# Own terms of two more units as TensorE products, decay rows first on two queues, and fewer idle products at the start

## The chip, the cores and the metric

The kernel runs on one core of one Trainium2 chip. The time is device microseconds of one execution; three runs of the kernel before took 583.14 to 583.82 us, with a median of 583.75. The engines are TensorE (PE, with its weight loads as PEld), VectorE (DVE), ScalarE (ACT), GpSimd (POOL) and SyncE (SP, which here only issues DMAs).

## What is computed

A recurrent attention block and, on its output, a dense block with the activation h - tanh(h):

```python
batch, n_heads, seq, head_dim = (4, 8, 768, 48)
for t in range(S):
    kt, vt, rt = (k[:, :, t], v[:, :, t], r[:, :, t])
    cur = np.einsum('bhd,bhe->bhde', u[None] * kt, vt)
    y[:, :, t] = np.einsum('bhd,bhde->bhe', rt, state + cur)
    state = w[None, :, :, None] * state + np.einsum('bhd,bhe->bhde', kt, vt)
...
n_tokens, d_model, d_ff = (3072, 384, 2048)
h = x @ w_in
g = h - np.tanh(h)
return (g @ w_out).astype(np.float32)
```

The term with `u` is the own term: the part of a step's output that comes from that step's own k and v.

## The kernel before

**Units.** The recurrence is cut into 24 units. Unit n covers a chunk of 64 steps (`SHORT`) of two of the four batches (`ch, half = divmod(n, 2)`), 128 rows in all. Per unit, r and k are transposed on PE (`turn`), scaled by powers of the decay w on DVE or ACT (`rT`, `kT`), and multiplied to a table `at` of step against step (`levels`, 16 products of 64x64). DVE copies the part before the diagonal into `at` by a mask (`x.cp`, line 830). The diagonal of `at` is the own term. PE then multiplies `at` by v (`outputs`), and `kw` (k times the decay to the chunk's end, `w_down`) by v to the new state (`to_state`). The result goes to `xt` and `rest`, the input of the dense block. The first two units have no state before them and take a shorter way.

**The own term has two ways.** Where `n < OWN` (line 32; OWN is 1), ACT scales `kT` by `w_u` in four operations (`own_k`, line 709), PE makes 16 products of it with `rT` (`own_levels`), and DVE copies their diagonal into `at` with the mask `same` (line 821). Else DVE makes `rk = r * k` (line 696), multiplies it by `ub`, a copy of u on all partitions (line 824), and sums it per head to `du` (line 700); ACT writes eight diagonals `same * du` into `at` (`diagonal`, line 704).

**The start.** w and u are loaded as eight short rows (`rows`, line 547) and transposed on PE into columns (line 549). ACT keeps a copy (`saved`, line 563). DVE makes the decay's powers from the columns: `by` (line 552), a scan to `power` (554), a reciprocal to `inverse` (558), which the scaling of r and k reads. `table` (line 529) transposes the inverse powers, and ACT makes `w_down` from it (562). POOL makes `w_u` and checks the bounds of w. `warm` (line 572) is an activation whose only use is that the table of ACT's functions is loaded. The weights come as 64-bit floating-point words in pieces of 768 KB (`st`) and are converted on DVE and ACT (lines 185 to 191).

**Idle products.** `fills` (line 534) are products of the identity with itself that write a bank which nobody reads: 512 columns for number 0, 256 for number 1, and the same two in another bank for numbers 2 and 3. They only keep PE busy.

**The dense block.** A block of two units gives 256 tokens; for each block and each pair of the 16 tiles of 128 columns of `w_in`, PE makes `h`, ACT and DVE make `g` from it by five activations (`th`, `s`, `sq`, `small`, `tg`) and three vector operations, and PE multiplies `g` by `w_out`, in the later passes by seven products instead of eight (`products`, line 307).

**What sets the order.** `lay_out` lists every piece of work as a task of one engine, and the string `ORDER` (line 45) names the tasks one by one, two characters each; numbers past the last task are idle products. `written` emits them in that order. So `ORDER` fixes what each engine, and each engine's DMA queue, does after what; an engine waits in place for what its next instruction needs.

Of the kernel before, what the change touches and what calls it, by code (L numbers as in the profile page):

```python
# [1279 lines left out]
```

## Time and profile before

| | |
|---|---|
| median of three runs | 583.75 us |
| the profiled execution | 583.45 us |
| its span, first instruction to last | 581.5 us |
| instructions | 14198 |
| granted TensorE clock, mean | 0.994 |
| PE busy | 567.1 us (98%) |
| DVE, ACT, POOL busy | 429.1, 403.5, 203.3 us |
| DMA | 38.48 MB |

The page of the profile gives the busy time of each engine and the chain of work that ended last: from the last instruction back to what released each one. In order of time, a row is: start, duration, engine, line, operation, out<-in, size, how many were merged, and in brackets the idle time before it with what ended it. Starts of neighbours on an engine are closer than their durations, since neighbours overlap. An idle product counts as busy time. A product of 32-bit numbers shows as two in the trace (x32 for 16 products of `levels`), a transpose as one.

### The profile page before, as it was taken

The numbers are of one execution on the slowest core, as the hardware profiler recorded it, in microseconds if no ns is written. First come the engines' busy times: TensorE is split into PE (matmuls) and PEld (weight loads), VectorE is DVE, ScalarE is ACT, GpSimd is POOL, SyncE is SP. The second block draws the span as 40 slices with busy tenths as digits, with TensorE's granted clock in tenths as the row PEclk, the third lists the DMA queues.
The fourth block names the chain that finished last, engine by engine and source line by source line (L and its number), as shares of the span: only waits on it lengthen the run. The fifth ranks groups of instructions, "written<-read, shape, count | busy, mean of one in ns | idle before, by whom it ended". The sixth has DMA issues, their size and how long they took to land.

```text
span 581.5 us, 14198 instructions
## 1 busy us (share of the span) xinstructions
PE 567.1 (98%) x5493; PEld 482.1 (83%) x5493; DVE 429.1 (74%) x720; ACT 403.5 (69%) x925; POOL 203.3 (35%) x366
## 2 busy tenths in 40 slices
PE   6899999999999999999999999999999999999997
PEld 3577777677777699999898889899899998989996
DVE  3799868699999989658789878686775564463545
ACT  2599899979777675637758776876776576765651
POOL 5003211110100144455357254446264344463340
PEclk7999999999999999999999999999999999999999
DMA  9966256776341001133343454423232010010001
GB/s 173 182 143 113 54 113 133 183 145 157 71 97 52 1 1 27 29 55 61 46 75 73 70 88 70 63 37 65 41 56 39 1 34 4 5 24 2 14 23 32
DMA packets 138548, 38.48 MB, mean 66 GB/s; under 512 B 130760, under 2 KB 132904, under 8 KB 138472
## 3 DMA queue, kind: packets, MB, share of 16 engines
q1 hardware_dynamic: 130140, 29.71, 27.9%
q0 software_dynamic: 4992, 6.99, 5.3%
q10 hardware_dynamic: 3340, 0.79, 0.8%
q8 instruction: 45, 0.74, 0.5%
q14 instruction: 31, 0.25, 0.1%
HBM read 31.66 MB, written 4.72 MB: 63 GB/s over the span
## 4 chain that ended last, share of the span: by engine, by line
PE 88%; DVE 4%; DMA 3%; ACT 2%; issue 2%; SPq 1%; POOL 1%; ACTq 0%; DVEq 0%
PE h L217 42%; PE p L307 27%; PE o L254 10%; PE yk_ps L606 6%; PE h L534 1%; PE x_ps L656 1%; SPq L644 1%; DMA vt<-in_v_dram 1%; DMA xt<-rest 1%; DMA first_k<-in_k_dram 1%; PE x_ps L606 1%; PE p L254 0%; ACT xt L765 0%; ACT rest L765 0%; DVE at L830 0%
## 5 line engine op out<-in xcount | busy, mean ns | idle before, releaser
L217 PE MATMUL h<-xt,w_in_sb 128*128 128x256 f32 x1152 | 266.4, 381 | 1.5 <-DMA xt<-rest 0.7
L217 PEld LDWEIGHTS h<-xt,w_in_sb 128*128 128x128 f32 x1152 | 214.9, 190 | 34.3 <-issue 2.3
L290 POOL TENSOR_TENSOR sg<-g 128x256 f32<-128x256 f32 x69 | 56.8, 824 | 169.8 <-DVE g L246 137.4
L242 DVE TENSOR_TENSOR g<-h,th 128x512 f32<-128x512 f32 x96 | 65.8, 686 | 60.2 <-ACT tg L233 29.1
L229 ACT ACTIVATE s<-h 128x512 f32<-128x512 f32 x96 | 57.3, 597 | 59.0 <-PE h L217 45.6
L307 PE MATMUL p<-mixed,sg 128*128 128x192 f32 x426 | 92.1, 326 | 0.0
L244 DVE TENSOR_TENSOR tg<-s,tg 128x512 f32<-128x512 f32 x96 | 69.1, 721 | 25.2 <-ACT s L224 17.7
L246 DVE COPY_PREDICATED g<-small,tg 128x512 f32<-128x512 int32 x96 | 73.0, 765 | 15.8 <-ACT small L235 12.9
L233 ACT ACTIVATE tg<-h 128x512 f32<-128x512 f32 x96 | 57.0, 594 | 33.0 <-PE h L217 29.0
L231 ACT ACTIVATE th<-h 128x512 f32<-128x512 f32 x96 | 56.5, 593 | 32.5 <-PE h L217 31.9
L307 PEld LDWEIGHTS p<-mixed,sg 128*128 128x128 f32 x426 | 73.5, 190 | 1.3 <-POOL sg L292 0.3
L307 PE MATMUL p<-w_out_sb,g 128*128 128x192 f32 x284 | 70.2, 329 | 0.0
L235 ACT ACTIVATE small<-s,smallb 128x512 f32<-128x512 f32 x96 | 68.5, 721 | 1.3
L254 PE MATMUL o<-w_out_sb,g 128*128 128x384 f32 x192 | 66.5, 489 | 0.5 <-DVE g L246 0.3
L786 POOL DMA_DIRECT2D xt<-rest x66 | 32.8, 502 | 94.7 <-ACT rest L765 94.7
L224 ACT ACTIVATE s<-s 128x512 f32<-128x512 f32 x96 | 60.3, 632 | 1.2
L254 PEld LDWEIGHTS o<-w_out_sb,g 128*128 128x128 f32 x192 | 35.6, 190 | 21.2 <-ACT parts L278 0.7
L307 PEld LDWEIGHTS p<-w_out_sb,g 128*128 128x128 f32 x284 | 50.7, 190 | 2.6
L704 ACT ACTIVATE at<-same,du 128x64 f32<-128x64 f32 x184 | 47.6, 341 | 6.5 <-PE yk_ps L606 5.0
L292 POOL TENSOR_TENSOR sg<-sg,g 128x128 f32<-128x128 f32 x69 | 39.4, 575 | 3.3
L294 POOL TENSOR_TENSOR sg<-sg,g 128x128 f32<-128x128 f32 x69 | 38.4, 561 | 3.9
L345 POOL DMA_DIRECT2D out_dram<-o x44 | 23.9, 545 | 39.8 <-DVE o L339 23.0
(126 smaller groups left out, 670.9 us busy)
## 6 DMA issues: line engine op xcount, KB each, us to landing
st<-in_moe_w_out_dram SPq DMA_DIRECT2D x8, 768.0 KB, 5.2
st<-in_moe_w_in_dram SPq DMA_DIRECT2D x16, 288.0 KB, 4.7
rt<-in_r_dram SPq DMA_DIRECT2D x46, 96.0 KB, 3.0
vt<-in_v_dram SPq DMA_DIRECT2D x46, 96.0 KB, 3.0
kt<-in_k_dram SPq DMA_DIRECT2D x44, 96.0 KB, 3.3
out_dram<-o POOLq DMA_DIRECT2D x44, 96.0 KB, 2.3
st<-in_moe_w_in_dram POOLq DMA_DIRECT2D x16, 96.0 KB, 5.5
parts<-in_k_dram SPq DMA_DIRECT2D x48, 32.0 KB, 2.2
```

Source lines behind the costliest of these rows:

```text
L217: self.nc.tensor.matmul(t.h2[:, z], self.w_in_sb[:, t.f // 2, kk, z * 128 : (z + 1) * 128], self.xts[t.j][:, kk].rearrange("p b t -> p (b ...
L224: A.activation(t.s, t.s, AF.Square, scale=G3)
L229: A.activation(out, t.h, AF.Arctan, scale=G2)
L231: A.activation(out, t.h, AF.Tanh)
L233: A.activation(out, t.h, AF.Tanh, scale=G1)
L235: A.activation(out, t.s, AF.Relu, bias=self.smallb, scale=-1.0)
L242: V.tensor_tensor(t.g, t.h, t.th, ALU.subtract)
L244: V.tensor_tensor(t.tg, t.s, t.tg, ALU.mult)
L246: V.copy_predicated(t.g, t.small.bitcast(I32), t.tg)
L254: self.nc.tensor.matmul(self.outs[i], t.g2[:, z, i * C : (i + 1) * C], self.w_out_sb[:, t.f + z, :], start=t.first and z == 0, stop=t.last ...
L290: add(t.s4[:, :2], g[:, 0::3], g[:, 1:2].to_broadcast([128, 2, C]), ALU.add)
L307: self.nc.tensor.matmul(ps[bank][:, half * n : (half + 1) * n], a, b, start=t.first and half == 0, stop=t.last, skip_group_check=True)
```

## The change

`OWN` goes from 1 to 3, and `ORDER` is replaced as a whole; nothing else is changed, except that all lines after it move up by one.

```diff
 PASSES = 4, 4, 8
-OWN = 1
+OWN = 3
 SWAP = 2
...
 ORDER = (
-    "0F2m2i2j2k2f2g2h00012l2n0J0K0G0H0IbWbW2q323133bX022o033534362t040A3738390C060U050B0T2s070V2rbWbWbWbW082u09bX2v2p"
...
+    "00010H2f2j2i2k2g2h0J2m2l2nbSbT020A030I040C060KbSbSbSbT2q0B2o3231333534362s050d072r2ubSbS2x2t0V2y2v082w090L3A0M2p"
...
```

With OWN at 3, units 1 and 2 take the first way of the own term, which unit 0 took already. The table has 18 idle fills before (nine of number 0, seven of 1, two of 2) and ten after (six of 0, three of 1, one of 3). Three places show the rest of what is moved; rows are in the order of the engine's program, without times.

At the very start, PE and ACT. `x_ps_146` is the bank of unit 0 and `x_ps_150` that of unit 1; `h<-ident` are fills. PE before, from its first instruction:

```order
L534 MATMUL h<-ident 128x512 x2
L656 MATMUL x_ps_146<-ident,first_k_122 128x128 x4
L534 MATMUL h<-ident 128x256
L549 MATMUL yk_ps<-ident,rows 128x8
L656 MATMUL x_ps_146<-ident,rt_106 128x128 x4
L534 MATMUL h<-ident 128x512 x4
L529 MATMUL h<-ident,twice 128x128 x4
L534 MATMUL h<-ident 128x256
L606 MATMUL x_ps_146<-rT,kU 64x64 x16
L566 MATMUL h<-one,ok 1x1
L606 MATMUL x_ps_146<-rT,kT 64x64 x16
L656 MATMUL x_ps_150<-ident,rt_107 128x128 x4
```

and PE now:

```order
L533 MATMUL h<-ident 128x512
L533 MATMUL h<-ident 128x256
L548 MATMUL yk_ps<-ident,rows 128x8
L533 MATMUL h<-ident 128x512 x3
L533 MATMUL h<-ident 128x256
L655 MATMUL x_ps_146<-ident,first_k_122 128x128 x4
L655 MATMUL x_ps_146<-ident,rt_106 128x128 x4
L533 MATMUL h<-ident 128x512 x2
L605 MATMUL x_ps_146<-rT,kT 64x64 x16
L605 MATMUL x_ps_146<-rT,kU 64x64 x16
L528 MATMUL h<-ident,twice 128x128 x4
L655 MATMUL x_ps_150<-ident,rt_107 128x128 x4
```

The transpose of w's and u's rows now comes before those of k and r, three fills and a half stand between them, two stand ahead of the levels, and none ahead of `table`. ACT before, from its first instruction (`L644` are loads of r, k and v):

```order
L644 DMA vt_116<-in_v_dram 64x8x48
L644 DMA first_k_122<-in_k_dram 64x8x48
L644 DMA rt_106<-in_r_dram 64x8x48
L547 DMA rows<-in_u_dram 4x2x48
L572 ACT_TABLE_LOAD
L572 ACTIVATE warm<-one 128x1
L644 DMA rt_107<-in_r_dram 64x8x48
L644 DMA first_k_123<-in_k_dram 64x8x48
L563 COPY saved<-yk_ps 128x8
L644 DMA vt_117<-in_v_dram 64x8x48
L560 COPY twice<-inverse 128x512
```

and ACT now:

```order
L546 DMA rows<-in_u_dram 4x2x48
L643 DMA first_k_122<-in_k_dram 64x8x48
L643 DMA rt_106<-in_r_dram 64x8x48
L643 DMA vt_116<-in_v_dram 64x8x48
L562 ACT_TABLE_LOAD
L562 COPY saved<-yk_ps 128x8
L643 DMA rt_107<-in_r_dram 64x8x48
L643 DMA first_k_123<-in_k_dram 64x8x48
L559 COPY twice<-inverse 128x512
```

The row of u is first on ACT's queue, as that of w is first on SP's (where `ub` was first before; it is now the 20th row there, after unit 2's loads). `warm` has left this place for a later one, the table load stands ahead of `saved`, and the second half of unit 1's v (`vt_117`) has moved behind a conversion of weights further down. `saved` also stands before `by` in the whole order now, after it before.

On DVE, from the scaled r of unit 0 to the masked copies of unit 1 (`at_132` is unit 0's table, `at_133` unit 1's; `same` is the mask of the own term). Before:

```order
L830 COPY_PREDICATED at_132<-before,x_ps_146 128x512
L807 TENSOR_TENSOR kw_113<-first_k_123,w_down 128x8x48
L696 TENSOR_TENSOR rk<-rt_107,first_k_123 128x384
L821 COPY_PREDICATED at_132<-same,x_ps_146 128x512
L189 SCALAR_TENSOR_TENSOR w_in_sb<-w_in_sb,st 128x768
L665 TENSOR_TENSOR kT<-x_ps_150,inverse 128x512
L660 TENSOR_TENSOR rT<-x_ps_150,power 128x512
L824 TENSOR_TENSOR rk<-rk,ub 128x384
L700 TENSOR_REDUCE du<-rk 128x8
L190 SCALAR_TENSOR_TENSOR power<-st,power 128x768
L191 TENSOR_TENSOR w_in_sb<-w_in_sb,power 128x768
```

and now:

```order
L820 COPY_PREDICATED at_132<-same,x_ps_146 128x512
L184 TENSOR_SCALAR power<-st 128x768
L185 TENSOR_SCALAR w_in_sb<-st 128x768
L806 TENSOR_TENSOR kw_112<-first_k_122,w_down 128x8x48
L806 TENSOR_TENSOR kw_113<-first_k_123,w_down 128x8x48
L664 TENSOR_TENSOR kT<-x_ps_150,inverse 128x512
L659 TENSOR_TENSOR rT<-x_ps_150,power 128x512
L188 SCALAR_TENSOR_TENSOR w_in_sb<-w_in_sb,st 128x768
L189 SCALAR_TENSOR_TENSOR power<-st,power 128x768
L829 COPY_PREDICATED at_133<-before,x_ps_150 128x512
L190 TENSOR_TENSOR w_in_sb<-w_in_sb,power 128x768
L184 TENSOR_SCALAR power<-st 128x768
```

`rk`, its product with `ub` and `du` are gone for unit 1; after the rows shown come one more conversion and unit 1's copy of the own term. Unit 0's `kw` has moved behind its two masked copies and the first steps of the conversion, which come in the same order as before.

On ACT at the first tile of the dense block, before (`at_132` here is unit 2's table):

```order
L704 ACTIVATE at_132<-same,du 128x64 x8
L233 ACTIVATE tg<-h 128x512
L231 ACTIVATE th<-h 128x512
L229 ACTIVATE s<-h 128x512
L224 ACTIVATE s<-s 128x512
L765 COPY xt<-yk_ps 64x3x64 x4
```

and now:

```order
L708 ACTIVATE kU<-kT,w_u 128x128 x4
L794 ACTIVATE state_127<-yk_ps,power 128x2x48 x4
L186 ACTIVATE power<-power,p_bias 128x768
L187 ACTIVATE st<-st 128x768
L230 ACTIVATE th<-h 128x512
L228 ACT_TABLE_LOAD
L228 ACTIVATE s<-h 128x512
L223 ACTIVATE s<-s 128x512
L234 ACTIVATE small<-s,smallb 128x512
L232 ACTIVATE tg<-h 128x512
L764 COPY xt<-yk_ps 64x3x64 x4
```

Unit 2's eight diagonals are four `kU`, a conversion's two steps and a second load of function tables have come between, and `small` has moved ahead of unit 2's `xt`. Everywhere else the same work stands in another order.

More of the change, by code (lines that the diff above doesn't have):

```diff
@@ new lines @@
+    "0N3C3T3B0D2z3S3U3E0O3D3738390P0S3J2+3G2_3Q0Q3K303H3P3R0R0e3F3V0f0T0U3I3q0g0E3ZbT3L0h3r3s3a3M0i3Y3o893c3n3p3b3d0j"
+    "3N0k3e3O0W3g3W3X0X3f4K0Y8A3h0F0Z3x4L4M8C3y4I0a8B3i4H4J3_8E0l0b8F8D3t400c3w3u3v3j4k8G8L153+4i3z0u3k418M4V423l4W44"
+    "434X4Y4l4m454h4j8H8ObV464R8P4O8I8N4S470m4Q4N4P8J0n3m485E4T8K8Q5B4C494U4v4F5C5D4Z4E4w4a4B4r0o5F5G4A4D4G4b4o0p134x"
+    "4c0w0q4y4s5c8T4d4q5f5P8Z5e5g5Q4e4t4n4p8a4u4f4z5R5b5d8S4+5S5L4g688b8l4_696A5T0r5H508e5I5J0s8R5K518U5M668m5N656752"
+    "6Z8V8d5A535O5p575i8c555q5U8f565l8n5r596V8W588q5V5hbW5j8p8h6Y6a5s8g5W6W6X8r8i5k8X545m5X8z5n6C6F735Y6J8+0t5o5Z7274"
@@ new lines @@
+    "5t6K6B6D5u6L8Y1D8t6M8j5v8_916E926G8o5w956N7S8s6_6j8k5x8u70716f7T7U8v5y6k5a905_6H8w6I605z9362948x647P6O8y96616c63"
+    "6l977Q7R6P6mJw7D6Q6n7E5+JxJy6e6b6d6R796g1L7d99Jt6h6S7eJuJv9A6i7F146T7G6U756o7H9N6p9D9B9E6q76779CKK9G7A6rKLKM7Z78"
+    "K5987f6sK69O7C7B6vKH7g6t6y0v9H6z7W7I7h6x6+9P9Z6w7JKq9FKIKJ9R9I7Y9Q127K7V7X9S9U6u7a7LK79J7b0x7M9a0y7c7N0zKV7iKW0+"
+    "9VJz9K9c7j9LKo0_9TJ+J_7k9d10KrKs9b9n9eKX119f9o7l9g1V16KnKp9z7m171TKS187u9W9+7s9h9M7p197t9X9p7r1AKY7q9i1U9YLB9r1E"
+    "9qKN1FA19jLCLD7O9s1BKOKP9_9k1G9u9v9tAB1C9mA29w1g1fAC9lA51HLh1h1M1WA39xK2A01NLE1OA49yLFLG1IADLiLjAEANA6AF1J1PAOAI"
@@ new lines @@
+    "AGAHAJAbAP1QARAc1KASAT1X1pA7AQKt1Y1R1e1ZA8AU1aAVAnA91bKZAKAoAA1SAfAeAL1xAqAiLkAdAWAMLlLmAg1cArAhA_K_1dApAsB0Au23"
+    "24AtAjM626BBAkB2KuKvB1Av25B4BCAwB31q0GAXB6BF1rBE1sBPBI1iAZB71tBQ1jBD1u1kAY1vB5BGBbB8Aa1w1lAlBT2P1mBSBcBH1nAm1oBe"
+    "BRLP2E2FBUAxBJ2G2HM5M7BKBdAyBgBWBf1yBVBXBpBhBYBiBq1z27B_AzBrA+Bt281+B9Bj1_BABs20Mc29C0MbMd21Bu2ABxBLBwBkCDBNC322"
+    "BvBMC12I2XC2CEC6BO2BCPCG2JCQ2C2KLQC4BZ2D2LByK8Ba2MCHC52NBlCFCKCSBm2QK92OCdC7BnCRBoCeCIC8CJ2YCUBz2ZCVCLCT2RB+2aCM"
+    "CW2bC97n2SCXCA2cCh2TCYCpCfCCCBCgCqCiCkLR2UCNCrCt2VCuCOCjCxCv2WCZCs2dCa2eD17zCwD2Cl85CmDGD4CcD5CbD3DH86CyCnD8DJDK"
@@ new lines @@
+    "81D6DV82DID9DL83DWD78788CoDXDADYDNDaCzDBDM7+DCDbDkC_DZDD84DlDO7vC+DcDdEADPD0DoDQ7_EBDmDpDEDsECDeDnED80DFDfDqDrEF"
+    "DTDREEEIEPDt7oEQDuL0DS7wDUETDgEGEHDiDhESL1DvEREWEeDwEUEVEXEfEJEYEKEtEgEhELEiEuElDjEvEjDxEZEwEmEkEaFJExEMEyE+EbEz"
+    "FK7xEnFYFLDzFND+FZFMD_E0FOE_DyF0ENFcE1EoE2FPE3FaEOFRFdFQEcFeF1E7FbFfFnE9FSF2LvFoE87yM_EpE4G0FpFgFqE6FrEdFhF3FsG1"
+    "FtE5FuEqFTGSG2G4FUG3ErG5G6EsF4G7FiG8F6FjGTF7F8FkF9FvF5GVGUFWFAGXFwFDGYGhFxFBG9FVGiFCFGFIFXGjGmFlGAGkGnFyFmGWFzGl"
+    "FEGZF+FFGoGBGaFHF_GpGDGbGqGcGwGCGFGGGdGEGHGeGIGxGJGKGLGfGMGzGPGyGOG_GgK0GQG+GrGuH2GNH1GsH9GRGtHAK1HbHBH0GvHDHCHc"
@@ new lines @@
+    "HEHGHFHHHqKQHdHIHeH3HrHfHJHgHiH4H7HhK4H5HtI3H6HuK3HsKRHvI4HxHjKAHyI5HkHwIII8HzHlKTH8HKHMHLLKH+HOI6HPHNHmKBI7HnHQ"
+    "IJKUKCHRIMIBILHSN0N1HoHTKDKxHVHUIAHpKEHYI9I1HZIKICH_INIkIPIOHaKFI0IQKwIlIDIRIzHWInKGHXImISIoI+IpIrITL2IEKyKaLLIF"
+    "I_J2JCK+L3KbI2IqIsJ1KcKzM9IGKdM8MAJ5ItLqIHJ0J3IuJ4JDKeJ6LwKlJRJGMJIUJFMKKkIVKfKiKgJ7IXLSIYIWIZKjIaLTJSKhIbIcIvIe"
+    "IwL4JVIdIhJ8JUJEIxLOIfJTKmJHIgIyJJJIIjL5JWJAIiJXJKJ9LNL6JZMEPFL7JYLsPGJaL8LxJLJBLyJMPULzJNLrPHJbPVPJJOPKJcPIJPJd"
+    "PXPMPLPNJQPYPOPWJeNWLMPPPbJgMePZPjPQNVNXPcMFJhPkJiL9PyPnPmPaPqLUPlJjPdJfMfMgLtPePzPfJkJlPgPSJnQ0PRJmPoN3P_PTPrLH"
```

60 lines of the change are left out of this document (17 added, 43 removed).

## The prediction

> **What bounds the kernel now.** I read the page first, then the stages of the span, then the first 50 us of each engine in order of time, since everything that the change names stands there.
>
> ```profile
> PE 567.1 (98%) x5493; PEld 482.1 (83%) x5493; DVE 429.1 (74%) x720; ACT 403.5 (69%) x925; POOL 203.3 (35%) x366
> ...
> PE 88%; DVE 4%; DMA 3%; ACT 2%; issue 2%; SPq 1%; POOL 1%; ACTq 0%; DVEq 0%
> ...
> st<-in_moe_w_in_dram POOLq DMA_DIRECT2D x16, 96.0 KB, 5.5
> ```
>
> TensorE (PE) is busy for 567.1 of 581.5 us, and 88% of the chain that ended last is its own work; so the end moves only by TensorE work that is taken away or by idle time of TensorE. The last row is for a rival below: an eighth of a weight piece (96 of 768 KB), issued by GpSimd (POOL), takes 5.5 us to land. The stages show where the idle time is.
>
> ```profile
> 0.00:15.00 15.00, 10.27 (x21) 4.72 (x22) 5.04 (x13) 3.55 (x8) 8.57 (x36) 0.79 0.99 173
> 15.00:30.00 15.00, 13.33 (x263) 9.09 (x262) 12.31 (x23) 7.37 (x19) 0.72 (x2) 0.99 1.01 196
> 30.00:45.00 15.00, 14.58 (x331) 11.00 (x330) 13.82 (x24) 14.49 (x44) 0.00 (x0) 1.00 0.59 115
> 45.00:60.00 15.00, 13.83 (x252) 10.68 (x252) 14.48 (x26) 14.67 (x47) 4.44 (x9) 1.00 0.65 108
> ```
>
> The columns are the stretch, its length, then busy us (and instructions) of PE, PEld, DVE, ACT, POOL, the granted clock, the DMA engines' share, and GB/s. PE idles 4.73 us in the first stage, 1.67, 0.42 and 1.17 us in the next three: 8.0 of the 14.4 us in all. From 30 us on DVE and ACT are nearly full too (ACT 14.49 and 14.67 of 15). In the first 30 us the DMA engines are full, but DVE and ACT are not (17.35 and 10.92 of 30 us): there a chain of waits sets the pace, and there the idle products, which count as busy, hide how little TensorE does.
>
> ```profile
> 9.57 0.24 PE L549 MATMUL yk_ps<-ident,rows 8*128 8x8 f32 x1 [2.48 <-issue]
> ...
> 10.65 5.99 PE L534 MATMUL h<-ident 128*128 128x512 f32 x8
> 16.47 0.60 PE L529 MATMUL h<-ident,twice 128*128 128x128 f32 x4
> ...
> 26.16 2.42 PE L534 MATMUL h<-ident 128*128 128x512 f32 x6
> 28.42 0.60 PE L656 MATMUL x_ps<-ident,kw 128*128 128x128 f32 x4
> 28.95 0.58 PE L606 MATMUL yk_ps<-at,vt 64*64 64x64 f32 x24
> ```
>
> The transpose that turns the rows of w and u into columns waits until 9.57; then come four idle fills of 512 columns, each of which shows as two products, until 16.47. Only then stands `table`, from which `w_down` is made. Unit 1's outputs, the last thing before the first tile's h, start at 28.95. The six idle products at 26.16 (four of 512 columns, two of 256, so five of 512) took 2.26 us to the next start, 0.45 for one at full clock.
>
> ```profile
> 2.24 0.72 ACTq L644 DMA_DIRECT2D rt<-in_r_dram  x1
> 4.98 1.23 ACTq L547 DMA_DIRECT2D rows<-in_u_dram  x1
> 6.24 1.28 ACT L572 ACT_TABLE_LOAD   x1 [6.24 <-issue]
> ...
> 13.72 1.28 ACT L709 ACTIVATE kU<-kT,w_u 128x128 f32<-128x128 f32 x4 [0.25 <-DVE kT L665]
> ...
> 33.40 2.04 ACT L704 ACTIVATE at<-same,du 128x64 f32<-128x64 f32 x8
> ```
>
> ACTq rows are DMA issues. The row of u left at 4.98, two us after the issue before it had ended (2.24 + 0.72); the table load follows it.
>
> ```profile
> 9.85 0.42 DVE L552 TENSOR_SCALAR by<-yk_ps 128x256 f32<-128x256 f32 x1 [7.70 <-PE yk_ps L549]
> ...
> 12.93 0.69 DVE L665 TENSOR_TENSOR kT<-x_ps,inverse 128x512 f32<-128x512 f32 x1
> ...
> 19.03 0.76 DVE L830 COPY_PREDICATED at<-before,x_ps 128x512 f32<-128x512 int32 x1
> 19.67 0.55 DVE L807 TENSOR_TENSOR kw<-first_k,w_down 128x384 f32<-128x384 f32 x1
> 20.13 0.56 DVE L696 TENSOR_TENSOR rk<-rt,first_k 128x384 f32<-128x384 f32 x1
> 20.60 0.72 DVE L821 COPY_PREDICATED at<-same,x_ps 128x512 f32<-128x512 int32 x1
> 21.21 0.94 DVE L189 SCALAR_TENSOR_TENSOR w_in_sb<-w_in_sb,st 128x768 f32<-128x768 uint32 x1
> 22.08 0.68 DVE L665 TENSOR_TENSOR kT<-x_ps,inverse 128x512 f32<-128x512 f32 x1
> 22.68 0.68 DVE L660 TENSOR_TENSOR rT<-x_ps,power 128x512 f32<-128x512 f32 x1
> 23.27 0.55 DVE L824 TENSOR_TENSOR rk<-rk,ub 128x384 f32<-128x384 f32 x1
> 23.86 0.55 DVE L700 TENSOR_REDUCE du<-rk 128x8 f32<-128x384 f32 x1
> ```
>
> From here the spacing of starts is used, since neighbours overlap: the first decay step 9.85 to `kT` 12.93 is 3.08; a masked copy into `at` 0.64 or 0.61; `kw` 0.46; a weight conversion 0.87; `kT` and `rT` 0.60 and 0.59. DVE has almost no pause from 19 us on: unit 1's outputs wait for its queue.
>
> **The sum, step by step.** It is made against the profiled execution, 583.45 us (span 581.5), 0.30 under the median of the three runs, 583.75.
>
> Step 1, rows first. Both row DMAs now open their queues, at about 1.2 us. By the old latency (4.98 to 9.57, behind other DMAs) the transpose comes at 5.8 at the latest. Another wait takes over: `warm` has gone from ACT's start, so the table load now stands ahead of the copy `saved`, behind four issues. 1.2 + 1.23 + 3 x 0.72 + 1.28 = 5.9, and 0.2 for the copy. That copy now comes before the first decay step in the program, and the step waits for ACT, with all of DVE's queue behind it. So the step starts at about 6.0, not 9.85, and `kT` of unit 0 could start at 9.1, not 12.93. `ub`, which stood first on SP, costs nothing where it goes: units 1 and 2 no longer read it, and unit 3's product, its first reader, comes at about 30 us.
>
> Step 2, idle products ahead of unit 0's transposes. They are now behind three fills and a half fill: seven 512-column products. What these take depends on the clock, for which the granted clock has rows:
>
> ```profile
> 5.20:8.60 3.40, 1.16 (x7) 0.69 (x6) 0.00 (x0) 1.49 (x2) 1.66 (x4) 1.00 1.03 229
> 8.60:12.00 3.40, 2.43 (x7) 1.76 (x8) 2.08 (x3) 0.17 (x1) 1.19 (x5) 0.50 1.31 184
> 12.00:15.40 3.40, 3.40 (x5) 1.35 (x4) 2.11 (x3) 1.90 (x5) 1.29 (x4) 0.50 1.26 187
> ```
>
> With PE busy 1.16 of 3.40 us, the clock fell to 0.50 for the next 6.8 us. At half clock a product took about 0.82 (eight took 5.82, the last two, after 15.4, at 0.45). So the seven take 3.2 to 5.7 us, and the eight transposes behind them about 0.9 (four took 0.44 at 16.47). From a transpose of w and u at 4.5 to 5.8 `kT` then starts between 9.1, where step 1 is last, and 12.9, no gain at all. Half clock to 8.6 and full after it gives 10.6 to 11.2; full clock from 5.2 on gives 9.1 to 10.1. I take 10.3, between the two. Lead so far 12.93 - 10.3 = 2.6.
>
> Step 3, from `kT` of unit 0 to unit 1's outputs: 28.95 - 12.93 = 16.0 before. Now two fills (four products, 1.8) and the levels (0.7, by 0.58 for 24 against 32) come first, 2.5 us; `table` no longer stands behind fills. Then DVE is the limit, by its new order: two masked copies 1.25, two weight steps and two more each about as `kw` (4 x 0.46), two `kw` 0.92, `kT` and `rT` 1.19, three conversions 2.61, a masked copy 0.64 and the new one of the own term 0.72: 9.2. Removed are unit 1's `rk`, its product with `ub` and the sum `du` (0.47 + 0.59 + 0.5), and ACT's eight diagonals. So 11.7 us, and the outputs start at 22.0: 4.3 more, lead 6.9. The own term's products on PE lie in the wait for DVE here and cost nothing; without that cover they would cost 0.7 (32 like the 24 above).
>
> Step 4, given back. The first tile's `s` needs another table than the first load brought, now that `warm` doesn't load it: a second load of 1.28 between `th` and `s`, where ACT is full (14.49 of 15), so at full price. Behind it are queued `s`, `tg`, unit 2's `xt` and `rest`, and PE's levels of unit 3. Unit 2's own products stand where PE is full: 0.7. ACT wins 2.04 - 1.28 = 0.76 there, four `kU` for eight diagonals. Sum 1.2; bounds 0 and 2.0.
>
> [...]
>
> Step 5, everything else. All other work has a new order too. Its cover is that PE is almost never idle after 60 us: 14.4 - 8.0 = 6.4 us, most of it at the very end, behind the last product. I take 0; it can win about 1.5 and lose as much.
>
> 6.9 - 1.2 = 5.7: 577.75 for the profiled execution, and with the 0.30 of the median **578.0**. Its own range, by the bounds of steps 3 to 5, is 576 to 580.
>
> **Rivals.**
>
> The clock falls once more: after unit 1's own products PE waits from about 19.6 to 22.0 for DVE, with one half fill in that wait where before there were several. That leaves about 1.2 busy of 3.4 us, like the row 5.20:8.60. Two stretches at half clock cost 2 x 1.7: 581.4. Against it: ACT and DVE are the limit right after, and hide some.
>
> [...]
>
> Slower: the clock stays low. With fewer idle products PE also waits at about 34 to 38 us for ACT. If no stretch between 22 and 42 us is busy enough to bring the clock back (2.43 of 3.40 busy at 8.60 did not, and the stretch after it, busy throughout, still ran at 0.50), six stretches cost 10.2 us: 583.75 - 5.7 + 10.2 = 588. It decides from the fourth stretch on (5.7 / 1.7). Against it: the h products fill whole stretches there.
>
> Weights late: GpSimd's last part of w_in's second piece now stands behind unit 1's v, half of which leaves on ACT's queue behind the first conversion, at about 13.8 by step 3. Two landings of 5.5 us, v's and then the part's, make 24.8, and DVE wants the piece at about 26.5. Full DMA engines (0.99 and 1.01) can make each landing two us longer; then DVE stands still for 2.3 us, and PE behind it: 580.3.
>
> The lead doesn't last: if DMA (0.99 and 1.01 of the first stages) and not the chain sets the pace, or ACT's full stages take the lead back, the time stays at 583.5. Against it: both begin earlier, and have 12.6 and 19 idle us of the first 30 to begin in.
>
> **How the numbers follow.** Forecast 0.58, clock once 0.14, weights late 0.09, no lasting lead 0.10, slower 0.09. A run of this kernel can tell about 0.2%, 1.2 us, from no change. Faster: 0.58 + 0.14 + 0.09 = 0.81; same 0.10; slower 0.09. The range holds the first three: from 575.8, with step 2 at its best (1.2 less) and 1.0 won in step 5, to 582.2, the clock rival with 0.8 for steps 4 and 5.
>
> **What would show it.** Right: the decay step on DVE near 6.0, `kT` of unit 0 at 9.1 to 11, unit 1's outputs near 22, the first tile's h near 24, two table loads on ACT with the second between `th` and `s`, the lead about 5.7 at unit 3's levels and the same at the end, PE's idle time after 60 us as before. Wrong: a granted clock of 0.50 after 20 us; DVE idle before the second piece's first conversion; a lead that shrinks stage by stage with ACT full. What would break the prediction is a wait in the new order after 60 us, of which nothing that I read tells.

## The result: 587.0 us, half a per cent slower, and the profile after

The changed kernel took 587.0 us (median of 8 runs, 585.06 to 588.82), the kernel before 583.17 beside it (median of 8, 581.68 to 584.07). The ratio is 1.0055, with a 95% interval of 1.0032 to 1.0077: slower, where 578.0 was forecast. The profiled execution took 586.18 us, span 584.5 (581.5 before). First the page (busy time, then the chain that ended last) and the first four stages, with the columns as before:

```profile
PE 563.5 (96%) x5541; PEld 483.3 (83%) x5541; DVE 423.3 (72%) x716; ACT 401.8 (69%) x918; POOL 197.5 (34%) x366
...
PE 86%; DMA 5%; ACT 4%; DVE 2%; issue 1%; POOL 1%; SPq 0%; ACTq 0%; DVEq 0%; POOLq 0%
```

```profile
0.00:15.00 15.00, 11.42 (x93) 6.21 (x93) 6.20 (x15) 3.25 (x7) 8.11 (x35) 0.99 0.92 165
15.00:30.00 15.00, 9.07 (x207) 7.19 (x207) 9.84 (x17) 6.51 (x15) 1.55 (x3) 0.61 1.08 174
30.00:45.00 15.00, 12.15 (x232) 9.88 (x231) 10.85 (x17) 11.87 (x28) 0.51 (x1) 0.94 0.80 159
45.00:60.00 15.00, 11.90 (x292) 9.38 (x293) 14.48 (x28) 14.61 (x48) 3.94 (x8) 1.00 0.47 94
```

The start is better than before, and everything from 15 to 60 us is worse: PE idles 5.93, 2.85 and 3.10 us in these stages (1.67, 0.42 and 1.17 before), the granted clock of the second is 0.61, and DMA has gone from 3% of the chain to 5%, ACT from 2% to 4%. Next ACT before (the two issues on which the reading rests), ACT now, and SP's queue now (three rows from the middle), in order of time:

```profile
6.32 0.65 ACTq L644 DMA_DIRECT2D rt<-in_r_dram  x1
7.01 0.65 ACTq L644 DMA_DIRECT2D first_k<-in_k_dram  x1
```

```profile
4.60 1.28 ACT L562 ACT_TABLE_LOAD   x1 [4.60 <-issue]
5.89 0.17 ACT L562 COPY saved<-yk_ps 128x8 f32<-128x8 f32 x1
10.83 0.60 ACTq L643 DMA_DIRECT2D rt<-in_r_dram  x1
11.47 0.78 ACTq L643 DMA_DIRECT2D first_k<-in_k_dram  x1
12.29 0.62 ACT L559 COPY twice<-inverse 128x512 f32<-128x512 f32 x1 [6.24 <-DVE at L829]
12.82 1.28 ACT L708 ACTIVATE kU<-kT,w_u 128x128 f32<-128x128 f32 x4
```

```profile
7.09 0.64 SPq L643 DMA_DIRECT2D first_k<-in_k_dram  x1
7.77 0.62 SPq L170 DMA_DIRECT2D st<-in_moe_w_out_dram  x1
8.44 2.61 SPq L643 DMA_DIRECT2D kt<-in_k_dram  x2
```

ACT issues the second half of unit 1's r at 10.83 and of its k at 11.47, where before they left at 6.32 and 7.01. Nothing that ACT computes comes between 6.06 and 12.29, though `inverse` was there at 9.07 (a reciprocal at 7.29, 1.78 long). `twice` starts when the issue ahead of it ends (11.47 + 0.78 = 12.25); the operation in its bracket only ended close to that. The program says why the issue came so late. Each transfer of SP and ACT here has one of eight counters (DMAHW0 to 7, the semaphores 101 to 108 of the trace), and in the trace each of their issues from 4.20 to 20.83 us waits for the counter that it takes. Four of SP's came 0.01 to 0.02 us after the landing of the transfer that had the counter (10.45 after 10.44, 11.23 after 11.21, 12.37 after 12.35, 12.95 after 12.94). The program's waits around ACT's issue:

```
ACT 6 L562 COPY saved_157<-yk_ps_142 128x8 [waits PE_49]
ACT 7 L643 DMA rt1_107<-in_r_dram 64x8x48 [waits DMAHW5_49]
ACT 8 L643 DMA first_k1_123<-in_k_dram 64x8x48 [waits DMAHW6_49]
ACT 9 L559 COPY twice_154<-inverse_153 128x512 [waits DVE_49]
SP  9 L170 DMA st_205<-in_moe_w_out_dram 128x2x384 [waits DMAHW4_49]
```

Counter 5 was that of ACT's half of unit 0's v, which landed at 10.81, 0.02 us before the issue. So ACT stands at that issue, with all its computing behind it, while SP runs ahead and puts 768 KB of w_out and two halves of unit 2's k before it, and half of unit 1's v before ACT's k. That half of k then takes 9.33 us, from 11.47 to 20.80. What PE and DVE make of it, PE first, with its last eight products (`p`) as the last row:

```profile
7.97 0.63 PE L655 MATMUL x_ps<-ident,first_k 128*128 128x128 f32 x4 [0.16 <-DMA first_k<-in_k_dram]
13.27 1.22 PE L605 MATMUL x_ps<-rT,kU 48*64 48x64 f32 x32 [1.90 <-ACT kU L708]
18.54 1.09 PE L655 MATMUL x_ps<-ident,rt 128*128 128x128 f32 x4 [3.13 <-DMA rt<-in_r_dram]
20.94 1.09 PE L655 MATMUL x_ps<-ident,first_k 128*128 128x128 f32 x4 [1.31 <-DMA rt<-in_r_dram]
28.31 0.92 PE L605 MATMUL yk_ps<-at,vt 64*64 64x64 f32 x24 [0.81 <-ACT power L186]
49.98 2.75 PE L253 MATMUL o<-w_out_sb,g 128*128 128x384 f32 x8
577.34 2.74 PE L253 MATMUL p<-w_out_sb,g 128*128 128x384 f32 x8
```

The last two rows before, for comparison, and then DVE now:

```profile
46.30 2.82 PE L254 MATMUL o<-w_out_sb,g 128*128 128x384 f32 x8 [0.24 <-DVE w_out_sb L191]
574.46 2.74 PE L254 MATMUL p<-w_out_sb,g 128*128 128x384 f32 x8
```

```profile
6.09 0.42 DVE L551 TENSOR_SCALAR by<-yk_ps 128x256 f32<-128x256 f32 x1 [3.94 <-ACT saved L562]
9.17 0.69 DVE L664 TENSOR_TENSOR kT<-x_ps,inverse 128x512 f32<-128x512 f32 x1
14.56 0.74 DVE L820 COPY_PREDICATED at<-same,x_ps 128x512 f32<-128x512 int32 x1 [2.33 <-PE x_ps L605]
20.90 0.56 DVE L806 TENSOR_TENSOR kw<-first_k,w_down 128x384 f32<-128x384 f32 x1 [4.22 <-DMA rt<-in_r_dram]
32.47 0.69 DVE L659 TENSOR_TENSOR rT<-x_ps,power 128x512 f32<-128x512 f32 x1 [2.60 <-ACT kT L691]
43.75 0.69 DVE L659 TENSOR_TENSOR rT<-x_ps,power 128x512 f32<-128x512 f32 x1 [1.09 <-ACT kT L691]
```

The decay step and `kT` of unit 0 are 3.76 us earlier than before, unit 1's outputs only 0.64, and the first product with w_out, `o`, is 3.68 us later (46.30 before). That last number is the whole result: from first `o` to the start of the last eight products it is 527.36 us (577.34 - 49.98), 0.80 less than before (574.46 - 46.30). The bracket at 20.90 names r, but `kw` reads k, whose second half landed at 20.80.

**How to read the stretch up to first `o`.** One window from the decay step to first `o`, for the kernel before, the changed one, and the best of the pure repairs below (a_sp1_warm); the third busy time, after the length and PE's and PEld's, is DVE's:

```profile
9.85:46.30 36.45, 34.11 (x608) 23.51 (x609) 31.62 (x53) 25.21 (x72) 3.20 (x10) 0.92 0.85 155
```

```profile
6.09:49.98 43.89, 31.87 (x659) 24.41 (x659) 30.68 (x49) 25.15 (x63) 4.88 (x13) 0.84 0.88 158
```

```profile
6.47:45.61 39.14, 30.33 (x660) 23.19 (x659) 30.42 (x49) 23.99 (x62) 4.76 (x13) 0.91 0.96 176
```

DVE has 30.4 to 31.6 us of work there in all three, and the rest is its idle time: 4.83 us before, 13.21 after, 8.72 in the repair. So first `o` moved by -3.76 (start) - 0.94 (work) + 8.38 (idle) = +3.68. With the 0.80 won behind it and 0.1 more at the very end this is the 3.0 of the spans.

### The profile page after: what moved, and what is told of

It is laid out like the page before. It is cut to its first block, busy times and chain, and to the rows that moved or that the text cites. A ratio compares the mean times of both kernels' runs of the same rounds, so it can differ in the third digit from the quotient of the medians.

```text
span 584.5 us, 14257 instructions
## 1 busy us (share of the span) xinstructions
PE 563.5 (96%) x5541; PEld 483.3 (83%) x5541; DVE 423.3 (72%) x716; ACT 401.8 (69%) x918; POOL 197.5 (34%) x366
## 4 chain that ended last, share of the span: by engine, by line
PE 86%; DMA 5%; ACT 4%; DVE 2%; issue 1%; POOL 1%; SPq 0%; ACTq 0%; DVEq 0%; POOLq 0%
PE h L216 42%; PE p L306 27%; PE o L253 9%; PE yk_ps L605 6%; DMA first_k<-in_k_dram 2%; DMA rt<-in_r_dram 1%; PE x_ps L655 1%; DMA kt<-in_k_dram 1%; DMA xt<-rest 1%; ACT at L703 1%; ACT xt L764 1%; PE x_ps L605 0%; PE p L253 0%; ACT kT L691 0%; DVE g L245 0%
## 5 line engine op out<-in xcount | busy, mean ns | idle before, releaser
L243 DVE TENSOR_TENSOR tg<-s,tg 128x512 f32<-128x512 f32 x96 | 67.6, 707 | 25.4 <-ACT s L223 13.5
L245 DVE COPY_PREDICATED g<-small,tg 128x512 f32<-128x512 int32 x96 | 71.2, 751 | 13.5 <-ACT small L234 11.1
L253 PEld LDWEIGHTS o<-w_out_sb,g 128*128 128x128 f32 x192 | 35.7, 190 | 20.5 <-DVE g L245 0.9
L703 ACT ACTIVATE at<-same,du 128x64 f32<-128x64 f32 x168 | 43.6, 340 | 1.8 <-DVE du L699 1.6
L291 POOL TENSOR_TENSOR sg<-sg,g 128x128 f32<-128x128 f32 x69 | 37.1, 543 | 3.3
L293 POOL TENSOR_TENSOR sg<-sg,g 128x128 f32<-128x128 f32 x69 | 35.1, 514 | 3.2
L306 PE MATMUL p<-w_out_sb,sg 128*128 128x192 f32 x142 | 34.8, 327 | 0.2 <-POOL sg L293 0.2
```

The source lines that it names most:

```text
L243: V.tensor_tensor(t.tg, t.s, t.tg, ALU.mult)
L245: V.copy_predicated(t.g, t.small.bitcast(I32), t.tg)
L253: self.nc.tensor.matmul(self.outs[i], t.g2[:, z, i * C : (i + 1) * C], self.w_out_sb[:, t.f + z, :], start=t.first and z == 0, stop=t.last ...
L306: self.nc.tensor.matmul(ps[bank][:, half * n : (half + 1) * n], a, b, start=t.first and half == 0, stop=t.last, skip_group_check=True)
```

## The experiments

Seventeen runs, all compared with the kernel before on the same chip. "First o" and "half" (time at half clock in the first 60 us) are from the one profiled execution, the time is the median, and the interval is 95%. The profiled execution can be any of a kernel's runs (the fastest of six for a_fills, the second slowest of twelve for a_sp1_warm), so first `o` doesn't order the medians closely: 47.05 stands beside 585.80 (b_own), 47.38 beside 583.97 (a_sp1_wout).

| run | edit | us | ratio to before | first o | half |
|---|---|---|---|---|---|
| after_again | changed kernel, unedited | 586.94 | 1.0049 [1.0024, 1.0075] | 50.94 | 17.1 |
| a_sp1 | unit 1's second halves issued by SP | 583.40 | 0.9987 [0.9969, 1.0005] | 46.23 | 6.8 |
| a_sp1_wout | the same, but behind w_out | 583.97 | 0.9987 [0.9965, 1.0008] | 47.38 | 10.2 |
| a_warm | one table load | 583.32 | 0.9978 [0.9961, 0.9994] | 45.22 | 3.4 |
| a_sp1_warm | a_sp1 and a_warm | 581.47 | 0.9958 [0.9940, 0.9975] | 45.61 | 6.8 |
| a_loads | w_in's first piece later | 585.29 | 1.0021 [1.0003, 1.0038] | 46.69 | 6.8 |
| a_late | w_out's load later | 586.26 | 1.0046 [1.0028, 1.0064] | 49.93 | 13.7 |
| a_wout | w_out's load and conversion later | 588.73 | 1.0072 [1.0048, 1.0095] | 53.24 | 17.1 |
| a_best | a_sp1_warm, a_loads, a_wout | 584.13 | 1.0006 [0.9987, 1.0025] | 47.32 | 10.2 |
| a_fills | five idle entries back | 588.13 | 1.0081 [1.0050, 1.0112] | 48.38 | 3.4 |
| a_own1 | a_sp1_warm, own terms as before | 582.07 | 0.9963 [0.9941, 0.9984] | 45.28 | 10.2 |
| a_keep | a_sp1_warm, two idle entries back | 580.89 | 0.9952 [0.9930, 0.9974] | 43.90 | 3.4 |
| b_rows | before, rows first | 585.14 | 0.9999 [0.9976, 1.0022] | 47.30 | 6.8 |
| b_own | before, own terms on PE | 585.80 | 1.0035 [1.0015, 1.0056] | 47.05 | 6.8 |
| b_both | before, both of these | 587.64 | 1.0064 [1.0042, 1.0086] | 50.46 | 10.2 |
| b_own_less | b_own, three idle entries fewer | 587.75 | 1.0064 [1.0041, 1.0086] | 50.48 | 10.2 |
| b_fewer | before, ten of 18 idle entries out | 583.64 | 0.9985 [0.9964, 1.0006] | 47.74 | 20.5 |

### Who issues unit 1's halves

```diff
-                of = [... for z, e in enumerate(("SP", "ACT" if n < L else "SP"))]
+                of = [... for z, e in enumerate(("SP", "ACT" if n < 1 else "SP"))]
```

> The changed kernel, with the second halves of unit 1's r, k and v issued by SP instead of ACT, at the same places of the order. Theory Q: the two issues that waited on ACT until 10.83 and 11.47 held the inverse's copies and kU behind them; now ACT's second step of the inverse starts near 9.3 (12.29) and kU of unit 0 near 10 (12.82), and unit 0's own term comes 2.5 to 3 us earlier; if r and k also land earlier, the whole is 1 to 4 us faster: 583 to 586. Theory D: the second halves still stand behind the weight piece and land at 18 or later, so unit 1 starts no earlier, and the whole stays within 1 us: 586 to 588. Theory C: 586 to 587.5.

583.40 us, ratio 0.9987: one changed condition takes back all that the change lost. From SP's queue of that run, and then from DVE:

```profile
7.49 1.28 SPq L643 DMA_DIRECT2D rt<-in_r_dram  x2
10.77 1.42 SPq L643 DMA_DIRECT2D first_k<-in_k_dram  x2
12.22 0.63 SPq L170 DMA_DIRECT2D st<-in_moe_w_out_dram  x1
```

```profile
15.55 0.74 DVE L820 COPY_PREDICATED at<-same,x_ps 128x512 f32<-128x512 int32 x1 [0.90 <-PE x_ps L605]
17.11 1.02 DVE L806 TENSOR_TENSOR kw<-first_k,w_down 128x384 f32<-128x384 f32 x2
```

The second half of k leaves about when it left before (11.41, against 11.47), but now w_out and unit 2's k leave behind it, and it lands at 15.66 instead of 20.80; ACT copies the inverse at 9.37 instead of 12.29. Two things went at once, the place among the transfers and the hold on ACT's computing. Theory Q had the time right and the way to it wrong: `kU` started at 12.29, not near 10, since half of unit 0's r landed late in this run (10.75; 7.39 in the changed kernel). Unit 0's own term was copied at 15.55, a us later than in the changed kernel, and still unit 1's outputs came 4.08 us earlier, for `kw` at 17.11 no longer waited. The next run keeps the waits and w_out's place, and takes away the hold (SP's rows):

```diff
 L643 DMA first_k1_123<-in_k_dram [waits DMAHW3_49]
+L170 DMA st_201<-in_moe_w_out_dram [waits DMAHW4_49]
 L643 DMA rt1_107<-in_r_dram [waits DMAHW5_49]
 L643 DMA first_k1_123<-in_k_dram [waits DMAHW6_49]
-L170 DMA st<-in_moe_w_out_dram
```

> The changed kernel with unit 1's second halves issued by SP, but now behind the first piece of w_out, so that each of the three waits for the same earlier transfer as in the changed kernel; ACT's computing is no longer held. Theory L (landing): what costs is that 768 KB of w_out are issued ahead of unit 1's k, which then lands at 17 to 20: first o 48.5 to 50.5, ratio to before 1.003 to 1.007, as the changed kernel. Theory H (hold): what costs is that ACT's issues, waiting, hold the inverse's copy and kU behind them; without it ratio 0.9975 to 1.0005, as with SP's issues ahead of w_out (0.9987, first o 46.23).

Ratio 0.9987 again: the weight piece ahead of the halves costs nothing that can be measured in the time, and theory L falls. But the edit took away more than the hold. Unit 2's k now stays behind unit 1's on SP's queue, and DVE's wait for k shrinks:

```profile
17.52 0.56 DVE L806 TENSOR_TENSOR kw<-first_k,w_down 128x384 f32<-128x384 f32 x1 [1.81 <-DMA first_k<-in_k_dram]
```

1.81 us against 4.22, since k's half lands at 17.42; and `kU` starts at 10.32 against 12.82. So the issue on ACT is the cause. Of its two effects the rows tell which one counts: k's landing. In the four runs named next k's half left between 11.41 and 11.55. With w_out, both halves of unit 2's k and a half of unit 1's v issued ahead of it, it landed at 20.80 (changed kernel) and 20.73 (a_late, below); with w_out alone at 17.42; with none of the four at 15.66. The hold on ACT's computing stretches DVE's wait ahead of unit 0's own term (2.33 us, against 0.90 in a_sp1), but DVE then stands idle for k until 20.90 anyway. No run keeps k's landing and takes away the hold alone. Two more runs move weights instead of the issue. In a_late SP's load of w_out stands behind unit 1's v:

```diff
-L170 DMA st<-in_moe_w_out_dram 128x2x384
 L643 DMA kt<-in_k_dram 64x8x48 x2
 L643 DMA vt_117<-in_v_dram 64x8x48
+L170 DMA st<-in_moe_w_out_dram 128x2x384
```

> The changed kernel with one load moved: the first piece of w_out leaves SP behind unit 1's r, k and v instead of ahead of unit 2's first k and unit 1's v. Its conversions on DVE stay where they were, ahead of w_in's second piece. Theory D: in the profiled run of the changed kernel 768 KB of w_out were issued at 7.77, ahead of the halves of unit 1's r and k that ACT issued at 10.83 and 11.47, and these landed at 18.54 and 20.80; without it they land 1.5 to 4 us earlier, and the whole is 2 to 4 us faster than the changed kernel, 583 to 585. Theory T (the table alone made the moved warm step 4 us faster): the place of w_out is worth under 1 us, 586 to 588.

586.26, no gain: theory D missed. ACT's half of unit 0's v landed at 10.80, unit 1's r left at 10.82, and k only at 11.48, after all four of SP's (w_out, the last of them, at 11.16):

```profile
10.82 0.63 ACTq L643 DMA_DIRECT2D rt<-in_r_dram  x1
11.48 0.71 ACTq L643 DMA_DIRECT2D first_k<-in_k_dram  x1
```

PE then waited 4.28 us for k, until 20.87. Unit 1's r had landed at 15.37, 3 us earlier than in the changed kernel, and that alone won nothing. In a_loads SP's two parts of w_in's first piece go behind r and k of units 0 and 1:

```diff
-L170 DMA st<-in_moe_w_in_dram 48x3x256
 L643 DMA rt_106<-in_r_dram 64x8x48
...
 L643 DMA first_k_123<-in_k_dram 64x8x48
+L170 DMA st<-in_moe_w_in_dram 48x3x256 x2
```

> The changed kernel, with SP's two parts of the first piece of w_in moved behind SP's parts of r and k of units 0 and 1; nothing else moves. Theory D (transfers): the 3.5 us by which the change is slower than was hoped for at 30 us come from the first 20 us of transfers, in which the weight piece stands ahead of unit 1's r and k. Then unit 1's last r lands by about 14 (18.54 in the changed kernel), its outputs come at 23 to 25 (28.31), and the whole takes 580 to 583. Theory C (clock): the loss is PE's work at half clock between 14.6 and 31.7, which this does not touch: 586 to 587.5. Theory Q (ACT's queue): r's second half stays on ACT and is issued only when its semaphore comes free, so it lands as late as now: 586 to 587.5, with the issue still near 10.8.

585.29, ratio 1.0021 against 1.0055: unit 0 was served sooner, so ACT's issue came at 7.37, k landed at 16.72, and about half of the loss went. None of the three expectations had this. In its profile PE also pauses for 1.79 us inside unit 1's own term (see the last section); whether that is the other half is not shown.

### The second table

```diff
+L571 ACT_TABLE_LOAD
+L571 ACTIVATE warm<-one 128x1
-L562 ACT_TABLE_LOAD
 L562 COPY saved<-yk_ps 128x8
```

> The changed kernel with the warm step (the one function of ACT that stands apart) moved to just ahead of the saved rows, so that ACT loads its table of functions once. Theory T (table): the second load, 1.28 us at 38.15 between two of ACT's steps that PE waits for, delays the rest by 1.0 to 1.4 us: 585.5 to 586. Rival: ACT has slack there, or the load moves to the start and delays the decay step by as much: 586.5 to 587.5.

583.32, ratio 0.9978: four us, three times the price of the load, and outside both expectations. But the edit did more than it says: in the program of this run the counters fall otherwise, r's half waits for counter 4 (unit 0's r) and w_out for 5. So w_out left at 10.91 instead of 7.77, unit 2's k behind unit 1's, and k's half landed at 17.30. The table was therefore tried where ACT issues nothing of unit 1:

> The changed kernel with two edits: unit 1's second halves of r, k and v issued by SP (alone 583.4, ratio to before 0.9987), and the warm step ahead of the saved rows, so that the table is loaded once (alone, with ACT's issue of unit 1's r waiting for another transfer than before, ratio 0.9978). Theory T+Q (two separate causes): the table's 1.28 us comes off what the first edit left, 582.0 to 582.6, ratio 0.9960 to 0.9970. Theory Q alone (the moved warm step helped because it changed which transfer ACT's issue waits for, and the table lies in slack): the same as with SP's issues alone, ratio 0.998 to 1.0005.

581.47: 0.9987 has become 0.9958, 1.7 us by the ratios and 1.9 by the medians, and the difference of two such ratios is known to about 1.5 us. That fits the 1.28 us of the second load and doesn't size it more closely; the rest of a_warm goes with k's landing. With both edits the change is faster than the kernel before, by 0.42%.

### Weights in another order

In a_wout the first piece of w_out stands behind w_in's second, its load and its conversions:

```diff
-L185 TENSOR_SCALAR w_out_sb<-st 128x768
 L188 SCALAR_TENSOR_TENSOR w_in_sb<-w_in_sb,st 128x768
+L185 TENSOR_SCALAR w_out_sb<-st 128x768
```

> The changed kernel with the first piece of w_out put behind w_in's second piece, its load on SP and its seven conversions on DVE and ACT, as in the kernel before. Theory W (weights in the wrong order): DVE spends 4.0 us on w_out ahead of w_in's second piece, and PE waits 1.22 before the third h (41.62 in the changed kernel) and 1.41 before unit 3's levels; without it the waits go, and the whole is 1.5 to 3 us faster than the changed kernel: 584 to 585.5. Rival: the load alone moved gave nothing (586.26), DVE has to do the 4 us of conversions ahead of the first o anyway, and unit 1's loads stay late: 586 to 587.

588.73, a miss. PE's wait before the third h grew from 1.22 to 2.16 us, that before unit 3's levels to 2.97, and first `o` came at 53.24: DVE had to convert both ahead of `o` anyway. The same two moves stand in a_best, the four edits together:

> The changed kernel with four edits together: w_in's first piece on SP behind r and k of units 0 and 1, unit 1's second halves on SP, the warm step ahead of the saved rows, and w_out's first piece behind w_in's second. If the causes are separate, their gains add to 5 to 8 us on the changed kernel: 578.5 to 582, ratio to before 0.991 to 0.9965. If they are one cause, the loads of unit 1, it stands where the best single edit stands, ratio 0.997 to 0.999.

584.13, ratio 1.0006, 2.7 us worse than a_sp1_warm alone and outside both expectations. Unit 1's outputs came at 23.12, but PE again waited 2.16 us before the third h, as in a_wout. The gains did not add.

### The two named edits in the order of before

b_rows moves only the rows to the head of both queues, b_own only changes the own terms (OWN = 3 and their tasks), b_both does both, and all 18 idle entries stay.

> The kernel before, its order kept, with the rows of w and u first on both queues; nothing else moves but their transpose, which PE then reaches ahead of unit 0's. Theory F (the head is bound by what is fed in): kT of unit 0 starts 2 to 3 us earlier (12.93 before), but its gain is used up at ACT's w_down and unit 1's chain: first h 1 to 2.5 us earlier than 31.59, whole 1 to 2 us faster. Rival: the loads that now stand behind the rows (first k and r of unit 0) come 0.8 to 1.3 later, the DMA engines are full anyway, and the first h stays within 0.7 us: whole the same within 0.7.

> The kernel before, its order kept, with the own terms of units one and two as TensorE products (own_k, products and masked copy in the place of the sums on VectorE and the diagonals on ScalarE); rows, loads and idle products as before. Theory of the prediction (the edit is good by itself): DVE loses 1.56 us of unit 1's sums and ACT 0.76, and what goes to PE (0.7 for each unit) lies in waits: unit 1's outputs come 1 to 1.5 us earlier (28.95 before), and the whole is 0.5 to 1.5 us faster. Rival: PE is the bound from 30 us on, so unit 2's 0.7 and the later place of its levels come back: within 0.7 us of the kernel before, on either side.

> The kernel before, its order kept, with both edits: rows first on both queues and the own terms of units one and two on TensorE; all idle products stay, and w_out still stands behind w_in's second piece. If the two named edits are good and the changed kernel's loss comes from its new order (weights ahead of unit 1's loads, idle products taken out of waits, two loads of tables), this is 1.5 to 3.5 us faster than the kernel before, with one load of tables. Rival: the edits themselves cost, then it is as slow as the changed kernel, 2 to 4 us slower than before.

b_rows: no change. The decay step starts at 5.44 instead of 9.85, and then DVE waits for PE, which waits for r:

```profile
10.71 1.09 PE L656 MATMUL x_ps<-ident,rt 128*128 128x128 f32 x4 [1.43 <-DMA rt<-in_r_dram]
```

b_own is slower by 0.35%, more than either expectation allowed. What stood beside the wait that it removes is still there, six idle products of 3.71 us at 24.36; unit 1's outputs start at 28.83 (28.95 before), and DVE stands still (a wait of 1.15 before):

```profile
33.44 0.69 DVE L660 TENSOR_TENSOR rT<-x_ps,power 128x512 f32<-128x512 f32 x1 [4.78 <-ACT kT L692]
```

b_both is as slow as the changed kernel, so the expectation that the named edits are good and only their order bad does not hold in this order. By the rows above, each edit uncovers the next wait. Taking the idle products out with the wait they had covered is b_own_less:

> The kernel before with the own terms of units one and two on TensorE (alone 585.8, ratio 1.0035), and three of the idle entries taken out that stood between unit 1's levels and its outputs, six products which took 3.71 us there. Theory P (own terms on PE are good once their wait is gone, and the idle products that covered the wait then cost): unit 1's outputs come 2 to 3 us earlier than in b_own (28.83), and the whole is 1.5 to 3 us faster than it: 582.5 to 584.3, ratio 0.998 to 1.001. Rival C (clock): without them the clock stays at half for one or two stretches more and gives the gain back: 585 to 587.

587.75, ratio 1.0064 against 1.0035 for b_own, with intervals that overlap: no gain, which is rival C's direction. The outputs came at 27.40, but the clock fell for 10.2 us while PE had real work, and 11 of the 12 products of the first h took 4.67 us (12 took 2.76 before):

```profile
33.02 4.67 PE L217 MATMUL h<-xt,w_in_sb 128*128 128x256 f32 x11 [0.40 <-issue]
```

### Idle products and the clock

b_fewer takes ten of the 18 idle entries out of the kernel before; a_fills puts five entries into waits of the changed kernel; a_keep puts one into each of two waits of a_sp1_warm (four products in the trace):

```diff
 L605 MATMUL yk_ps<-at_132,extra_130 64x64 x12
+L533 MATMUL h<-ident 128x512
 L605 MATMUL x_ps_150<-rT,kT 64x64 x16
 L605 MATMUL yk_ps<-vt_116,kw_112 64x48 x16
+L533 MATMUL h<-ident 128x512
```

> The kernel before with 8 of its 18 idle entries: three at the start, two of the four ahead of the table, one between there and unit 1, and the two of the late bank; all else is as before. Theory C: the idle products kept the clock at full in most runs of the kernel before; without ten of them PE's share falls below what the clock needs at 20 to 30 us, it stands at half for 7 us or more, and the whole is 1 to 4 us slower: ratio 1.002 to 1.007. Rival: they stand in waits and do nothing: within 0.7 us, ratio 0.9988 to 1.0012; or they cost where their waits are short, and it is 1 us faster.

> The changed kernel with five idle products put back: two behind the table, and one each behind unit 1's r transposes, its levels and its own products. Theory C: the granted clock stood at half for 13.7 us between 14.6 and 31.7 because PE waited too much; with products in these waits it stays at full for at least half of that, and the whole is 2 to 4 us faster: 583 to 585. Theory D or Q: PE waits for loads there, not for its clock, and the whole moves by under 1 us: 586 to 588.

> The kernel with SP's issues and the early warm step (ratio 0.9958), with two idle entries put back just where PE waited there: two products behind unit 0's outputs (1.46 us idle) and two behind its products into the state (1.38 us idle). Theory C (the clock, once the loads come in time): each fits its wait at 0.8 us, the clock stays at full through 30 us (it stood at half from 23.11 to 29.94), and the whole is 1 to 2.5 us faster: ratio 0.9915 to 0.994. Rival: the half clock there lies beside DVE's conversions, which PE waits for anyway, and nothing is won: ratio 0.995 to 0.9975.

b_fewer stood at half clock for 20.5 us of its first 60 and lost nothing (0.9985). Its longest stretch fits that: PE had 9.72 us of work in 13.65, even at half clock, and DVE 11.16.

```profile
21.57:35.22 13.65, 9.72 (x131) 7.99 (x124) 11.16 (x19) 10.09 (x30) 0.00 (x0) 0.50 0.93 183
```

a_fills, 588.13, missed both expectations and decides nothing about theory C. Its profile (3.4 us at half) is of the fastest of its six runs, 584.62, in which w_out happened to leave at 11.00 and k's half to land at 18.57. The three runs with a mean granted clock of 0.994 or 0.995 took 584.62 to 587.39, the three with 0.986 to 0.989 took 588.87 to 591.26. Against theory C, that the changed kernel lost by its clock, stand b_fewer and the table, where time at half clock doesn't order the runs (10.2 us at 0.9963 in a_own1, 6.8 us at 1.0035 in b_own). That the clock costs a part in the order of the changed kernel is not excluded. a_keep, with the loads in time, is the fastest of all, 580.89, but its ratio cannot be told from that of a_sp1_warm; its rival stands. Last, the own terms back on DVE and ACT in the order of a_sp1_warm, and the control:

> The kernel with SP's issues and the early warm step (ratio to before 0.9958), with the own terms of units one and two put back: sums on DVE, diagonals on ACT, no own products on PE; u in every row's form is loaded on SP behind unit 1's k, since they need it. Theory P (own terms on PE pay): unit 1's outputs come 1 to 2.5 us later (23.85 there), DVE carries 1.56 us more for each unit, and the whole is 0.5 to 2 us slower: ratio 0.9967 to 0.9993. Theory O (they cost, as in the order of before, where they alone gave 1.0035): PE has 1.3 us less of its own work and the whole is 0.5 to 2 us faster: ratio 0.9925 to 0.995.

> The changed kernel itself, unedited, on the same chip as the three runs beside it, so that they have one reference: ratio 1.003 to 1.008 if it stands as before (1.0055).

a_own1 is 582.07, ratio 0.9963 against 0.9958: where the loads come in time, it can't be told whether the own terms on PE pay or cost, and both theories forecast more. The control is 1.0049.

## Why the prediction was wrong

**Step 1 was right:** the decay step at 6.09 (6.0 forecast). **Step 2 was better than forecast:** the clock stayed at full to 14.6, and `kT` started at 9.17 (10.3 forecast). In a_sp1, a_warm and a_sp1_warm it was 11.49, 11.14 and 11.04, since half of unit 0's r landed later; the row that sets it is then a transfer, not an idle product. So the early `kT` here was in part luck.

**Step 3 failed, by 6.3 us:** outputs at 28.31, 22.0 forecast; from `kT` on it took 19.14 us where the sum had 11.7. "DVE is the limit, by its new order" added up DVE's work and never asked when unit 1's r and k land: DVE stood idle for 8.21 of the 19.14 us, 4.22 of them for k. The order of ACT was quoted with the two issues behind `saved`, and step 1 read it only as far as `saved`. Shown: with these issues on SP the outputs come at 24.23 (a_sp1) and 23.85 (a_sp1_warm), 12.74 and 12.81 us after `kT` with 2.05 us of idle time in each, and the loss is gone. Where k lands in time, the sum is thus off by 1.1 us only. The rival "weights late" looked at one moved transfer, the weights, and not at the r and k of the next unit.

**Step 4 failed too.** From unit 1's outputs to first `o` it took 21.67 us, 17.35 before: 4.3 given back, where the sum had 1.2. The table load was priced well (1.28 in its row, and 1.7, give or take 1.5, in the time). It starts at 38.15, 0.02 us after `th` ended at 38.13, and the next activation starts at 39.44, 0.01 us after its end, so its row holds all of its cost on ACT. That the own terms' 0.7 and 0.76 cancel fits a_own1. But the lead did not last: in a_sp1_warm, with one table load, the outputs lead by 5.1 us and first `o` by 0.69; in a_keep by 6.45 and 2.40. Of a_sp1_warm's 4.4 us 3.8 are more idle time of DVE (5.00 against 1.18 before), most of it in waits for ACT's copy of `kT` and for PE:

```profile
28.02 0.69 DVE L659 TENSOR_TENSOR rT<-x_ps,power 128x512 f32<-128x512 f32 x1 [2.62 <-ACT kT L691]
32.92 0.74 DVE L820 COPY_PREDICATED at<-same,x_ps 128x512 f32<-128x512 int32 x1 [1.40 <-PE x_ps L605]
```

The forecast took the lead at unit 1's outputs as the lead at the end, less some prices. But the end hangs on first `o`, ahead of which DVE has 30.4 to 31.6 us of work: by an estimate from the rows, the earliest `o` without any idle time is 6.1 + 30.7 = 36.8 at the changed kernel's start, and a new wait of DVE there delays it. That also bounds what the change could have won.

**Step 5 was right:** 0.80 won, 1.5 allowed either way.

**The rivals.** 588 was forecast for a clock that stays low, and 587.0 came, with the clock at half for 13.7 us. But that rival kept step 3's outputs and lost 10.2 us to the clock; here the outputs were late by k's landing, and 20.5 us at half clock cost b_fewer nothing. The near number is luck. "The lead doesn't last: DMA sets the pace" named the right place, at 583.5, and did not see that it can go below zero. The one slower case, the clock's, had 9%, and its 588 lay above the range of 575.8 to 582.2, which should have reached it.

## What to carry to other kernels

When a start is moved earlier, don't carry the lead down one chain: take the engine whose fixed work fills the stretch up to the stage on which the end hangs, and ask for each of its waits whether it stays. Read each moved transfer to its end, with the earlier one that its issue waits for, and with what the other queue sends ahead of it meanwhile: here it helped to put the waiting issue on the queue of those later transfers, so that they stayed behind it (a_sp1, ratio 0.9987 against 1.0055). Don't count on idle products: ten of 18 entries fewer cost nothing here (b_fewer, ratio 0.9985).
